# Six stretches of an attention and two-FFN kernel: instructions moved by a place or two

## Chip, core and metric

One core of a Trainium2 chip runs the whole program. The metric is the device time of one execution in microseconds (us), from the first to the last instruction with the launch's own share around it. The times of the kernel before are 1404.84, 1405.35 and 1405.74 us, median 1405.35.

## What is computed

The core of the reference, with B = 8 sequences of S = 512 tokens and 32 states, 8 heads of 64:

```python
scores = scale * x @ state.T;  a  = softmax(scores);  xread = a @ state
scores2 = scale * state @ x.T; a2 = softmax(scores2); sread = a2 @ x
x = concat([xread, sread]) as (4352 rows, 512)
h = silu(x @ w_gate) * (x @ w_val);  x = h @ w_out          # 1536 hidden columns
h = x @ w_in2;  g = max(h, 0) + alpha * min(h, 0)           # 2048 hidden columns
out = g @ w_out2
```

The weights come as float64 and are converted on the chip. Every product is made of three passes on a number's rounded high part and its remainder (`PASSES`: high times high, high times low, low times high), so each value that enters a product is first split: ScalarE copies it rounded (`acopy`, L78), then VectorE subtracts the copy from it (`sub_lo`, L84). A matmul here is 128x128 weights against 512 columns, or 256 for the states.

## The kernel before, in words

**Order of the work.** TensorE follows the order of the code everywhere. Up to the last token block the other engines and the DMA queue are ordered by the framework's planner, which goes by priority and its own costs, and by edges written by hand: `with tc.issue_after(ins)` puts what the block issues on the engine of `ins` behind `ins`. From the states' block on (L1265), VectorE, ScalarE, GpSimd and the SP queue follow the code too. Each engine works its queue in order.

**The attention and the first FFN.** The rows of one sequence are a block; the 256 state rows make a ninth, the states' block. Its inputs are read from attention by `second_read` (L217): 32 small matmuls into one of the two `aux` banks of PSUM. The product of state and weights (`state_times_w`, L508) also goes to the two `aux` banks and is split from there. `gate(f)` and `value(f)` are products for 128 hidden columns (12 of them, f = 0 to 11), in banks `g` and `v`; ScalarE reads `g` for the Silu (L547), VectorE multiplies by `v` (L551). `split(f)` (L554) makes the two parts, `project(f)` (L569) adds the result to the banks `acc0` to `acc3`.

For the first two blocks (XT = 2) all gates and values come first (the `order` loop, L769 to L792, with the list `extra` saying what is put after the gate or value of each number n), then a second loop (L809 to L821) splits and projects. Meanwhile `stream1` converts the weights in units. A unit has `act` (ScalarE, L268 and L269), `bits` (VectorE, L275 and L277, through a PSUM bank as scratch, then GpSimd L282 or L285) and, for w_out1, `uses` (the split into `wp`, L78 and L84). `banks` (L274) names the scratch bank: `acc0` and `acc1` for w_gate, w_val and the first three units of w_out1, `g` and `v` for the last three. Counting the steps, the fourth unit's `bits` are issued in the `order` loop, after the value products of the last number: half 0 after the first of its two values, half 1 after the second. The later units' are issued in the second loop.

**The states' block.** `ffn1` (L586) runs f = 0 to 11 with places (f, 0) after the gate, (f, 1) after the value and (f, 2) after the projection. For this block `split(f - 1)` stands at the head of f. `split_w(f + 2)` (L737), 1024 columns on ScalarE and VectorE, is at (f, 0). `x2_pair` (L907) prepares the inputs of the second FFN's first pair of blocks: four loads at (1, 2), four subtractions and seven 1024-column splits, two to a place, up to (6, 2).

**The second FFN.** It goes by pairs of blocks with seven products in place of eight (`FORMS`). A step t makes the seven products of one pair of hidden columns (`hidden_pair`, L974); after each comes a place (`fill`, L1217), which also takes one link of earlier steps: six matmuls of the output product (`project`, L1086, L1096). The first link into a sum is copied from its bank by ScalarE (L78, `sum<-acc`), the others are added by VectorE (L1107). A pair has ten such first links, in the steps t = 8p + 2 and 8p + 3 and the first place of 8p + 4. A link's bank is written again by the next link of its chain, two links later.

The first two steps are begun inside the states' block: two products for each f from `FROM` = 7 on, at (f, 0) and (f, 2), so ten of the fourteen; the other four follow the block's last projection. From f = `FROM` the block's own gate and value use `acc2` and `acc3`.

```python
copy = s == 0 and (pr, to, e) not in put_in
...
if copy:
    put_in.add((pr, to, e))
    acopy(r, o)
else:
    nc.vector.tensor_tensor(out=r, in0=o, in1=r, op=ALU.add)
```

Of the kernel before, what the change touches and what calls it, by code (L numbers as in the profile page):

```python
# [8 lines left out]
F32 = mybir.dt.float32  # L9
# [16 lines left out]
def attention_and_two_ffns(ctx: ExitStack, tc: tile.TileContext, x, state, w_gate, w_val,  # L26
# [220 lines left out]
    class Unit:  # L247
# [23 lines left out]
        def bits(self, i):  # L271
            m = self.m[i] = t2([P, HALF], I32, "m32")
            lo, hi = self.words(i)
            t = psum([P, HALF], self.banks[i]).bitcast(I32) if self.banks else m  # L274
            nc.vector.tensor_scalar(out=t, in0=hi, scalar1=0x0FFFFFFF, scalar2=3, op0=ALU.bitwise_and,  # L275
                                    op1=ALU.logical_shift_left)
            self.made = nc.vector.scalar_tensor_tensor(  # L277
                out=m, in0=hi, scalar=-0x80000000, in1=t, op0=ALU.bitwise_and, op1=ALU.bitwise_or)
            if self.place:
                o = self.place(i)  # L280
                n = o.shape[-1]
                nc.gpsimd.tensor_tensor(out=o.bitcast(I32), in0=m.rearrange("p (a n) -> p a n", n=n),  # L282
                                        in1=lo.rearrange("p (a n) -> p a n", n=n), op=ALU.add)
            else:
                nc.gpsimd.tensor_tensor(out=m, in0=m, in1=lo, op=ALU.add)  # L285
# [90 lines left out]
    def unit_w(j, c):  # L376

        def place(k):
            if j not in wraw:
                wraw[j] = t8([P, NPAIR, 2, 2 * P], F32, "wr")  # L380
            return wraw[j][:, c:c + 2, k, :]
        return Unit([words(w, c, c + 2, 2 * P * j, 2 * P * (j + 1)) for w in (w_gate, w_val)], place,
                    banks=("acc0", "acc1"))

    def unit_o(j):
        def take(i, m):
            if j not in wo1:
                wo1[j] = t8([P, 2, 2, DM], F32R, "wp")
            acopy(wo1[j][:, i, 0], m)
            sub_lo(wo1[j][:, i, 1], m, wo1[j][:, i, 0])  # L390
        return Unit([words(w_out1, 2 * j, 2 * j + 2, 0, DM)], take=take,
                    banks=("acc0", "acc1") if j < EARLY else ("g", "v"))
# [124 lines left out]
    class Block:  # L517
# [36 lines left out]
        def split(self, f):  # L554
            p = self.p.pop(f)
            t = self.hid[f] = t4([P, 2, S], F32R, "h")
            acopy(t[:, 0, :self.n], p)
# [28 lines left out]
    def ffn1(blk, slots, before):  # L586
# [5 lines left out]
        for f in range(NF1):  # L592
            if f and blk.n < S:
                blk.split(f - 1)
# [8 lines left out]
            elif before:  # L603
                before()
                if blk.n < S:
                    blk.start()
            fill(f, 2)
# [3 lines left out]
    with tc.manual_schedule(engines={mybir.EngineType.PE}):  # L611
# [67 lines left out]
        def ffn1_slots(b):  # L679
# [15 lines left out]
            if b == B - 1:  # L695
                put(0, 2, lambda: nc.sync.dma_start(alpha_sb, alpha.rearrange("(k p) -> p k", p=P)))
                gen = load_xs()
                for f in range(4, 8):
                    put(f, 0, lambda: next(gen))
                put(NF1 - 3, 1, lambda: split_w(0))  # L700
# [42 lines left out]

        blocks = [block(b) for b in range(B)]
# [10 lines left out]
        def columns(t):  # L755
            t.scores()
            with tc.issue_after(units1[3].made.ins):
# [5 lines left out]
                 2: [[att[0, g].second_scale for g in range(NG)], [att[0, 0].second_read],  # L763
                     [att[0, 1].second_read], []],
                 3: [[att[1, g].second_scale for g in range(NG)], [att[1, 0].second_read],
                     [att[1, 1].second_read], []]}
# [42 lines left out]
        for b in range(XT):  # L809
            for f in range(NF1):  # L810
# [3 lines left out]
                if b == 0:  # L814
                    with tc.issue_after(values[-1].ins):
# [90 lines left out]

        def x2_pair(pr):  # L907

            r, x = {}, x2.setdefault(pr, {})

            def load(c, d):
                r[d, c] = t4([P, 2, S], F32, "x2r")
                nc.sync.dma_start(r[d, c], x2d[2 * pr + c][:, 2 * d:2 * d + 2, :])

            def sub(o, x0, x1):
                nc.vector.tensor_tensor(out=o, in0=x0, in1=x1, op=ALU.subtract)

            def first():
                r["t1"] = t4([P, 2, S], F32, "x2t")
                sub(r["t1"], r[0, 1], r[0, 0])  # L920

            def put(k, src):
                x[k] = split8(r[src])

            return [lambda: [load(c, d) for d in range(2) for c in range(2)], first,
                    lambda: put("b00", (0, 0)),
                    lambda: sub(r[0, 0], r[1, 1], r["t1"]),
                    lambda: put("t2", (0, 0)), lambda: put("t1", "t1"),
                    lambda: sub(r[0, 1], r[1, 1], r[0, 1]),
                    lambda: put("t3", (0, 1)),  # L930
                    lambda: put("b10", (1, 0)),
                    lambda: sub(r[1, 0], r[1, 0], r[0, 0]),
                    lambda: put("t4", (1, 0)), lambda: put("b11", (1, 1))]
# [134 lines left out]
        acc, sums, put_in, giving, turning, sending, soon = {}, {}, set(), [], [], [], []  # L1068

# [16 lines left out]
        def project(gr, n, e):  # L1086
# [16 lines left out]
            if copy:  # L1103
                put_in.add((pr, to, e))
                acopy(r, o)
# [101 lines left out]
        def step(t, pr, s):  # L1207
# [7 lines left out]
            places = [0]  # L1215

            def fill():  # L1217
                places[0] += 1
                for e in list(sending):
# [42 lines left out]
        FROM = 7  # L1262
        forming, work = {}, [lambda: None for _ in range(2 * 7 + 1)]
        E = mybir.EngineType
        with tc.manual_schedule(engines={E.DVE, E.Activation, E.Pool, E.SP}):  # L1265


            slots = {}
            for f in range(2, NF1):
                slots.setdefault((f - 2, 0), []).append(lambda f=f: split_w(f))  # L1270
            for i, th in enumerate(x2_pair(0)):
                slots.setdefault((1 + i // 2, 2), []).append(th)
            slots.setdefault((4, 2), []).append(lambda: [ahead() for _ in range(3)])
# [10 lines left out]
            blk.split(NF1 - 1)  # L1284
# [42 lines left out]
```

## Time and profile before

| what | value |
|---|---|
| median of 3 runs | 1405.35 us (1404.84 to 1405.74) |
| profiled execution, its own time | 1406.81 us |
| span of its instructions | 1405.0 us |
| TensorE busy | 1361.7 us (97%) |
| VectorE busy | 1037.8 us (74%) |
| ScalarE busy | 827.5 us (59%) |
| GpSimd busy | 556.7 us (40%) |
| granted TensorE clock, mean | 0.993 |

The time of the profiled execution is 1.81 us more than its span, and 1.46 us more than the median. An engine that is busy for nearly the whole span sets the time; what can be won without changing its work is the time in which it waits, and the time in which it runs at the lower clock. In a timeline a row is a start, a duration, the engine, the line, the operation with the names of its output and inputs, how many such instructions in a row, and in brackets the engine's idle time before it with what ended that time. In a table of stretches the columns after the length are the busy us of TensorE, its weight loads, VectorE, ScalarE and GpSimd, each with its number of instructions, then the granted clock as a share of full speed.

### The profile page before, as it was taken

How to read it: one execution, taken by the hardware profiler on the slowest of the kernel's cores; microseconds unless marked ns; L12 is line 12 of the kernel's file. 1: busy time of each engine (PE TensorE's matmuls, PEld its weight loads, DVE VectorE, ACT ScalarE, POOL GpSimd, SP SyncE). 2: the span in 40 equal slices, each digit the busy share in tenths (PEclk: the TensorE clock that was granted, in tenths of full speed). 3: DMA queues.
4: the chain of work that ended last, by engine and by line, in shares of the span. 5: the costliest groups of instructions: out<-in, count | busy, mean ns of one | idle time of the engine just before them, and what ended most of it. 6: DMA issues, size and time to landing. Idle time of an engine off the chain costs nothing.

```text
span 1405.0 us, 20644 instructions
## 1 busy us (share of the span) xinstructions
PE 1361.7 (97%) x7238; PEld 1066.8 (76%) x7238; DVE 1037.8 (74%) x1593; ACT 827.5 (59%) x1440; POOL 556.7 (40%) x422
## 2 busy tenths in 40 slices
PE   6899999999999999999899999999999999999997
PEld 3566777777767677777897888878888888888886
DVE  6778535877777777765656789888897889888651
ACT  6756425555555555553456757776676667666642
POOL 3432111312222312320025666566566656656611
PEclk8999999999999999999999999999999999999999
DMA  9442333575757657533507688679868896886792
GB/s 299 158 138 49 85 78 91 160 183 160 208 135 222 173 138 210 153 113 105 190 21 254 181 303 273 199 205 327 291 201 226 299 314 224 218 263 219 266 316 94
DMA packets 274480, 271.92 MB, mean 194 GB/s; under 512 B 133960, under 2 KB 198472, under 8 KB 273352
## 3 DMA queue, kind: packets, MB, share of 16 engines
q1 hardware_dynamic: 272232, 270.21, 63.1%
q8 instruction: 57, 0.93, 0.3%
q10 hardware_dynamic: 2144, 0.39, 0.2%
q14 instruction: 47, 0.39, 0.1%
HBM read 206.05 MB, written 64.49 MB: 193 GB/s over the span
## 4 chain that ended last, share of the span: by engine, by line
PE 79%; DVE 7%; POOL 4%; issue 3%; ACT 3%; DMA 3%; SPq 0%; POOLq 0%; DVEq 0%; ACTq 0%
PE acc L1096 17%; PE acc L575 17%; PE g L534 9%; PE v L534 9%; PE v L984 7%; PE aux L984 5%; PE g L984 5%; PE aux L500 3%; POOL u L996 2%; PE acc L1166 2%; DVE h L84 1%; POOL u L953 1%; PE aux L163 1%; PE aux L223 1%; DMA wo<-ws2d 1%
## 5 line engine op out<-in xcount | busy, mean ns | idle before, releaser
L1096 PE MATMUL acc<-h,wo 128*128 128x512 f32 x1344 | 341.6, 390 | 2.6 <-ACT sum L78 1.5
L575 PE MATMUL acc<-h,wp 128*128 128x512 f32 (+1 forms) x1296 | 298.1, 380 | 7.3 <-DVE h L84 5.3
L1096 PEld LDWEIGHTS acc<-h,wo 128*128 128x128 f32 x1344 | 251.2, 188 | 56.8 <-ACT sum L78 2.7
L575 PEld LDWEIGHTS acc<-h,wp 128*128 128x128 f32 x1296 | 235.0, 189 | 57.5 <-DVE h L84 7.3
L953 POOL TENSOR_TENSOR u<-u,m 128x512 f32<-128x512 f32 x96 | 128.7, 1341 | 300.1 <-ACT m L952 267.8
L84 DVE TENSOR_TENSOR h<-u,h 128x512 fp32r<-128x512 f32 x160 | 151.6, 964 | 24.1 <-ACT h L78 23.8
L534 PE MATMUL g<-a,sw 128*128 128x512 f32 x576 | 153.7, 401 | 3.6 <-ACT h L78 1.7
L78 ACT ACTIVATE h<-u 128x512 fp32r<-128x512 f32 x160 | 100.2, 630 | 89.3 <-POOL u L996 88.0
L534 PE MATMUL v<-a,sw 128*128 128x512 f32 x576 | 151.5, 398 | 0.7 <-DVE p L551 0.5
L534 PEld LDWEIGHTS g<-a,sw 128*128 128x128 f32 x576 | 103.9, 188 | 62.2 <-issue 33.5
L984 PE MATMUL v<-x,w 128*128 128x512 f32 x576 | 146.5, 390 | 0.1
L1107 DVE TENSOR_TENSOR sum<-acc,sum 128x512 f32<-128x512 f32 x184 | 125.4, 682 | 22.7 <-PE acc L1096 21.9
L534 PEld LDWEIGHTS v<-a,sw 128*128 128x128 f32 x576 | 105.2, 188 | 32.9 <-issue 8.9
L984 PEld LDWEIGHTS v<-x,w 128*128 128x128 f32 x576 | 107.8, 188 | 22.7 <-DVE u L992 0.5
L84 DVE TENSOR_TENSOR h<-h,h 128x512 fp32r<-128x512 f32 (+1 forms) x80 | 79.2, 991 | 42.4 <-ACT h L78 40.0
L317 POOL TENSOR_TENSOR m<-m,raw 128x512 int32<-128x512 int32 x32 | 46.3, 1447 | 156.4 <-DVE m L315 115.7
L996 POOL TENSOR_TENSOR u<-u,u 128x512 f32<-128x512 f32 x64 | 105.5, 1648 | 5.0
L84 DVE TENSOR_TENSOR sw<-aux,sw 128x512 fp32r<-128x512 f32 x96 | 62.7, 684 | 57.6 <-ACT sw L78 57.4
L78 ACT ACTIVATE sw<-aux 128x512 fp32r<-128x512 f32 x96 | 52.6, 595 | 86.6 <-PE aux L500 79.3
L952 ACT ACTIVATE m<-m,alpha_sb 128x512 f32<-128x512 f32 (+1 forms) x144 | 99.2, 689 | 0.0
L984 PE MATMUL g<-x,w 128*128 128x512 f32 x384 | 97.7, 390 | 0.7 <-ACT h L951 0.7
L984 PE MATMUL aux<-x,w 128*128 128x512 f32 x384 | 97.6, 390 | 0.0
(158 smaller groups left out, 2098.8 us busy)
## 6 DMA issues: line engine op xcount, KB each, us to landing
wo<-ws2d SPq DMA_DIRECT2D x224, 256.0 KB, 5.1
w<-w2d SPq DMA_DIRECT2D x104, 512.0 KB, 5.4
w2d<-sp SPq DMA_DIRECT2D x32, 512.0 KB, 4.0
x2r<-x2d SPq DMA_DIRECT2D x25, 512.0 KB, 5.8
w<-w2d SPq DMA_DIRECT2D x48, 256.0 KB, 5.5
x2d<-xo SPq DMA_DIRECT2D x32, 256.0 KB, 2.6
raw<-in_moe_w_in_dram SPq DMA_DIRECT2D x16, 512.0 KB, 4.0
raw<-in_moe_w_out_dram SPq DMA_DIRECT2D x16, 512.0 KB, 4.7
```

Source lines behind the costliest of these rows:

```text
L78: return nc.scalar.activation(o, i, AF.Copy)
L84: (eng or nc.vector).tensor_tensor(out=o, in0=src, in1=hi.bitcast(F32), op=ALU.subtract)
L317: nc.gpsimd.tensor_tensor(out=m, in0=m, in1=lo, op=ALU.add)
L500: nc.tensor.matmul(self.o[Ns * c:Ns * (c + 1), :], stt[b][q, 2 * c + g, :], wraw[j][q, c].rearrange("p k f -> p (k f)"), start=True, stop= ...
L534: nc.tensor.matmul(o[:, :self.n], self.lhs(f, k, a, which), self.rhs(k, c), start=(i == 0), stop=(i == last))
L575: nc.tensor.matmul(self.acc[e][:, :self.n], wo1[f // 2][:, f % 2, a, e * P:(e + 1) * P], t[:, c, :self.n], start=(self.n == S and f == 0 a ...
L952: nc.scalar.activation(n, n, AF.Copy, scale=alpha_sb[:, f:f + 1])
L953: nc.gpsimd.tensor_tensor(out=out, in0=out, in1=n, op=ALU.add)
L984: nc.tensor.matmul(o, w[:, a, q], x[k][:, q, e], start=start and n == 0, stop=stop and n == 5, skip_group_check=True)
L996: nc.gpsimd.tensor_tensor(out=o, in0=x0, in1=x1, op=ALU.subtract)
L1096: nc.tensor.matmul(o, w[:, f, a, e], h[:, q], start=first and i == 0, stop=i == 5, skip_group_check=True)
L1107: nc.vector.tensor_tensor(out=r, in0=o, in1=r, op=ALU.add)
```

## The change

Six stretches are touched, named here by the order of the run.

1. Second reads: for n = 2 and 3 of the first loop, the two `second_read` stand one entry later in `extra`.
2. Conversion banks: `banks` becomes a function of the half, asked when `bits` is issued. For w_out1 it gives `acc0` and `acc1` as long as the first block has no accumulators, else `g` and `v`.
3. Conversion order: in the second loop, what a conversion step issues on ScalarE goes behind the rounded copy of that turn's `split(f)`.
4. States' block: the four loads go to place (5, 0) of the last token block and the four subtractions to (7, 2) to (10, 2) there, with three tiles more; the seven splits stand one to a place, (0, 2) to (6, 2); `split_w(f + 2)` goes from (f, 0) to (f, 1); `split(f)` goes from the head of f + 1 to before (f, 2); the first loads of w2 go from (4, 2) to (3, 2).
5. First products: `FROM` is 6, so twelve of the fourteen products of the first two steps are inside the states' block.
6. First sums' copies: those in places 4 to 7 of a step go to VectorE (five of a pair's ten, twenty in all).

```diff
-            t = psum([P, HALF], self.banks[i]).bitcast(I32) if self.banks else m
+            t = psum([P, HALF], self.banks(i)).bitcast(I32)
...
-                    banks=("acc0", "acc1"))
+                    banks=lambda i: f"acc{i}")
...
-                    banks=("acc0", "acc1") if j < EARLY else ("g", "v"))
+                    banks=lambda i: f"acc{i}" if blocks[0].acc is None else ("g", "v")[i])
...
-            acopy(t[:, 0, :self.n], p)
+            self.rounded = acopy(t[:, 0, :self.n], p)
...
         for f in range(NF1):
-            if f and blk.n < S:
-                blk.split(f - 1)
             blk.gate(f)
...
+            if blk.n < S:
+                blk.split(f)
             fill(f, 2)
...
+                put(5, 0, first_load)
+                for i in range(4):
+                    put(7 + i, 2, lambda i=i: first_sub(i))
...
+        def first_load():
+            for d in range(2):
+                for c in range(2):
+                    raw0[f"b{d}{c}"] = t4([P, 2, S], F32, "x2r")
+                    nc.sync.dma_start(raw0[f"b{d}{c}"], x2d[c][:, 2 * d:2 * d + 2, :])
+
+        def first_sub(i):
+            x0, x1, to = (("b01", "b00", "t1"), ("b11", "t1", "t2"), ("b11", "b01", "b01"), ("b10", "t2", "t4"))[i]
+            o = raw0[to] if to in raw0 else t4([P, 2, S], F32, "x2t")
+            nc.vector.tensor_tensor(out=o, in0=raw0[x0], in1=raw0[x1], op=ALU.subtract)
+            raw0["t3" if to == "b01" else to] = o
...
-                 2: [[att[0, g].second_scale for g in range(NG)], [att[0, 0].second_read],
-                     [att[0, 1].second_read], []],
+                 2: [[att[0, g].second_scale for g in range(NG)], [], [att[0, 0].second_read],
+                     [att[0, 1].second_read]],
...
                 if b == 0:
-                    with tc.issue_after(values[-1].ins):
+                    with tc.issue_after(values[-1].ins), tc.issue_after(blocks[b].rounded.ins):
                         stream1.until(2 * NJ1 + f // 2, 2)
...
-                acopy(r, o)
+                (vcopy if where[0] > 3 else acopy)(r, o)
...
-        FROM = 7
+        FROM = 6
...
             for f in range(2, NF1):
-                slots.setdefault((f - 2, 0), []).append(lambda f=f: split_w(f))
-            for i, th in enumerate(x2_pair(0)):
-                slots.setdefault((1 + i // 2, 2), []).append(th)
-            slots.setdefault((4, 2), []).append(lambda: [ahead() for _ in range(3)])
+                slots.setdefault((f - 2, 1), []).append(lambda f=f: split_w(f))
+            for i, k in enumerate(FORMS):
+                slots.setdefault((i, 2), []).append(lambda k=k: x2[0].update({k: split8(raw0.pop(k))}))
+            slots.setdefault((3, 2), []).append(lambda: [ahead() for _ in range(3)])
```

(The entry of n = 3 is changed like that of n = 2; `where[0]` is the place of the step, set in `fill`; `x2_pair` is taken out.)

## Rows read from the trace of the kernel before

**Rows 1.** The page, part 1: busy time of the engines, whole run.

```profile
PE 1361.7 (97%) x7238; PEld 1066.8 (76%) x7238; DVE 1037.8 (74%) x1593; ACT 827.5 (59%) x1440; POOL 556.7 (40%) x422
```

**Rows 2.** TensorE's waits: waiting line, releaser, total us, times, longest us.

```profile
PE aux L155 <- DMA xn<-in_x_dram: 7.9, 4, 5.4
PE acc L575 <- DVE h L84: 5.3, 5, 3.2
PE aux L223 <- DVE sw L84: 3.0, 2, 1.5
```

**Rows 3.** Timeline round the first second read, VectorE and TensorE.

```profile
59.83 1.29 DVE L84 TENSOR_TENSOR sw<-aux,sw 128x512 fp32r<-128x512 f32 x2 [0.95 <-ACT sw L78]
60.58 0.66 PE L223 MATMUL aux<-xn,e2t 128*32 128x64 f32 x32 [1.48 <-DVE sw L84]
```

**Rows 4.** Timeline, VectorE and TensorE round conversion of w_out1's fourth unit.

```profile
126.98 0.68 DVE L277 SCALAR_TENSOR_TENSOR m<-raw,g 128x512 int32<-128x512 int32 x1
...
127.80 1.62 PE L534 MATMUL g<-a,sw 128*128 128x512 f32 x6 [1.67 <-ACT h L78]
...
130.64 16.48 PE L575 MATMUL acc<-h,wp 128*128 128x512 f32 x72
...
134.58 0.68 DVE L277 SCALAR_TENSOR_TENSOR m<-raw,v 128x512 int32<-128x512 int32 x1
```

**Rows 5.** Timeline, ScalarE and TensorE in the first block's projections.

```profile
147.69 0.63 ACT L78 ACTIVATE wp<-m 128x512 fp32r<-128x512 f32 x1 [2.26 <-POOL m L285]
148.22 3.89 ACT L78 ACTIVATE h<-p 128x512 fp32r<-128x512 f32 x7
...
148.89 0.50 PE L575 MATMUL acc<-h,wp 128*128 128x512 f32 x1 [1.76 <-ACT h L78]
149.70 20.72 PE L575 MATMUL acc<-h,wp 128*128 128x512 f32 x83 [0.30 <-DVE h L84]
```

**Rows 6.** Stretches of 25 us: busy us (instructions), clock, DMA share, GB/s.

```profile
150.00:175.00 25.00, 25.00 (x103) 19.61 (x102) 14.14 (x24) 10.61 (x18) 1.42 (x1) 0.93 0.19 64
...
675.00:700.00 25.00, 20.80 (x169) 20.20 (x168) 17.26 (x22) 12.96 (x20) 0.00 (x0) 1.00 0.70 236
...
1025.00:1050.00 25.00, 25.00 (x112) 20.72 (x111) 24.21 (x31) 15.72 (x26) 19.34 (x13) 1.00 0.73 218
```

**Rows 7.** Timeline, states' block: VectorE, then TensorE.

```profile
683.09 1.23 DVE L916 TENSOR_TENSOR x2t<-x2r,x2r 128x1024 f32<-128x1024 f32 x1 [4.40 <-DMA x2r<-x2d]
684.23 0.42 DVE L84 TENSOR_TENSOR h<-s,h 128x256 fp32r<-128x256 f32 x1
684.56 1.22 DVE L84 TENSOR_TENSOR ws<-wr,ws 128x1024 fp32r<-128x1024 f32 x1
...
684.70 1.58 PE L575 MATMUL acc<-h,wp 128*128 128x256 f32 x11 [3.16 <-DVE h L84]
...
699.22 1.58 PE L575 MATMUL acc<-h,wp 128*128 128x256 f32 x11 [0.91 <-DVE h L84]
```

**Rows 8.** Timeline, TensorE from the first products to the first sums.

```profile
724.38 1.58 PE L575 MATMUL acc<-h,wp 128*128 128x256 f32 x11 [0.73 <-DVE h L84]
...
750.33 1.67 PE L984 MATMUL g<-x,w 128*128 128x512 f32 x6 [0.74 <-ACT h L951]
...
755.18 0.73 PE L1096 MATMUL acc<-h,wo 128*128 128x512 f32 x2 [0.88 <-DVE h L84]
```

**Rows 9.** Timeline, first sums of the first two pairs, TensorE and VectorE.

```profile
771.25 1.65 PE L1096 MATMUL acc<-h,wo 128*128 128x512 f32 x6 [0.35 <-ACT sum L78]
...
923.11 0.89 DVE L84 TENSOR_TENSOR h<-u,h 128x512 fp32r<-128x512 f32 x1 [1.69 <-ACT h L78]
...
925.41 1.66 PE L1096 MATMUL acc<-h,wo 128*128 128x512 f32 x6 [1.14 <-ACT sum L78]
```

**Rows 10.** The page, part 5: VectorE groups, count, busy us, mean ns, idle.

```profile
L84 DVE TENSOR_TENSOR h<-u,h 128x512 fp32r<-128x512 f32 x160 | 151.6, 964 | 24.1 <-ACT h L78 23.8
...
L1107 DVE TENSOR_TENSOR sum<-acc,sum 128x512 f32<-128x512 f32 x184 | 125.4, 682 | 22.7 <-PE acc L1096 21.9
```

More of the change, by code (lines that the diff above doesn't have):

```diff
@@ L742, in split_w @@
             ws[f] = t
+        raw0 = {}
+        def first_load():
[8 more added lines that the diff above has]
+            raw0["t3" if to == "b01" else to] = o
         blocks = [block(b) for b in range(B)]
@@ L762, in attention_and_two_ffns @@
                  1: [[v.first_scale], [u.first_parts], [v.first_parts], []],
-                 2: [[att[0, g].second_scale for g in range(NG)], [att[0, 0].second_read],
-                     [att[0, 1].second_read], []],
-                 3: [[att[1, g].second_scale for g in range(NG)], [att[1, 0].second_read],
-                     [att[1, 1].second_read], []]}
+                 2: [[att[0, g].second_scale for g in range(NG)], [], [att[0, 0].second_read],
+                     [att[0, 1].second_read]],
+                 3: [[att[1, g].second_scale for g in range(NG)], [], [att[1, 0].second_read],
+                     [att[1, 1].second_read]]}
         order = [(0, 0), (0, 1), (1, 0), (1, 1)] + [(b, j) for j in range(2, NJ1) for b in range(XT)]
@@ L905, in x2_forms @@
             return places
[L907 to L933, printed above, removed]
         def x2_last():
@@ L1068, in attention_and_two_ffns @@
         acc, sums, put_in, giving, turning, sending, soon = {}, {}, set(), [], [], [], []
+        where = [0]
         def store(u, o):
@@ L1215, in step @@
             places = [0]
+            where[0] = 0
             def fill():
                 places[0] += 1
+                where[0] = places[0]
                 for e in list(sending):
@@ L1268, in attention_and_two_ffns @@
             slots = {}
+            x2[0] = {}
             for f in range(2, NF1):
-                slots.setdefault((f - 2, 0), []).append(lambda f=f: split_w(f))
-            for i, th in enumerate(x2_pair(0)):
-                slots.setdefault((1 + i // 2, 2), []).append(th)
-            slots.setdefault((4, 2), []).append(lambda: [ahead() for _ in range(3)])
+                slots.setdefault((f - 2, 1), []).append(lambda f=f: split_w(f))
+            for i, k in enumerate(FORMS):
+                slots.setdefault((i, 2), []).append(lambda k=k: x2[0].update({k: split8(raw0.pop(k))}))
+            slots.setdefault((3, 2), []).append(lambda: [ahead() for _ in range(3)])
             first = (_ for t in range(2) for _ in step(t, *STEPS[t]))
@@ L1283, in attention_and_two_ffns @@
             ffn1(blk, slots, lambda: blocks[B - 1].finish(B - 1))
-            blk.split(NF1 - 1)
             blk.finish(B)
```

## The prediction

> **What bounds it now.** I read the page first: TensorE is busy for 1361.7 of 1405.0 us [rows 1]. The change neither adds nor takes away a matmul, so it can win only from TensorE's 43 idle us and from time at the lower clock. The second view is therefore TensorE's list of waits. Its largest entry, 7.9 us for the first loads of x, lies at the start, which the change leaves alone; the projections' wait for VectorE (5.3 us in five) and the second reads' (3.0 us in two) lie where it moves things [rows 2]. Third, the timeline at each such wait, to see which instruction the late one stood behind in its queue. VectorE and ScalarE are seldom full, so these are questions of order: a short instruction that TensorE needs stands behind a long one that could wait.
>
> **Part 1, second reads.** The read writes an `aux` bank. Both banks hold the states' products until VectorE has split them, 1.29 us for two from 59.83; TensorE stands 1.48 us before the read at 60.58 [rows 3], and as long again for the second sequence (3.0 us in two [rows 2]). With the reads one place later, a gate product of 1.6 us (its like in [rows 4]) runs in that gap: the products before end some 59.1 (60.58 less 1.48), the gate then ends at 60.6, and the first bank is free about 60.5, half-way through the two splits. The read becomes as late as the bank, so I keep 0.03 us of each wait: 2.9 us won, between 0 and 2.96. The value products after it need nothing that comes later than before.
>
> **Part 2, conversion banks.** Only the fourth unit of w_out1 gets other banks, since `bits` of the later ones come when the accumulators exist. Its first half has its scratch in `g`, between two gates: VectorE reads `g` until 127.66 (126.98 and 0.68) and the gate starts at 127.80 after 1.67 us [rows 4]. The profile names ScalarE's copies as the releaser; by the end times it is VectorE. In `acc0` that half no longer stands in the gate's way: 1.67 us won. The bound on the other side is the second half: today it ends at 135.26 (134.58 and 0.68) after the last value. In `acc1` it has to end before the first projection writes that bank, three matmuls of 0.23 us (16.48 by 72) after a start that moves to 128.97, so at 129.66. If the planner leaves it where it is, TensorE waits 5.6 us. I take 1.67, because the unit's data are ready long before and its bank is then free; 5.6 is the first rival.
>
> **Part 3, conversion order.** At 146 to 150 TensorE waits 1.76 and 0.30 us for the seventh turn's split. ScalarE makes that copy only at 148.22, in a run of seven, directly after a conversion copy at 147.69 that itself waited 2.26 us for GpSimd [rows 5]. Seven copies in a row mean that their buffers had long been free. The edge puts each turn's copy ahead of that turn's conversion instructions: 2.06 us won, between 0 and 2.06. What the edge makes later is the last unit's `act` and the `uses` of three units. They have room: the last of these copies was made at 147.69, and the first projection that needs its unit is the eleventh, four turns of 2.75 us (12 by 0.229) after the seventh, which stood at 148.89 [rows 5].
>
> Behind this wait the granted clock falls: 0.93 over 150 to 175 and 103 matmuls, where a full-speed stretch of the same length shows 112 of the like size [rows 6]. That is 7% of 25 us, 1.75 us at 1.2 in place of 2.4 GHz, and I take 1.7 as won with the wait, between 0 and 1.75. Against it: after the wait of 3.16 us at 681 the stretch shows a clock of 1.00 [rows 6, 7], so not every pause of this length costs clock. The Trainium skill (TensorE: Matmul & The Clock Gate, Part 1) says the gate looks at activity in a window that runs on its own, whatever the kernel does. By that, a pause may or may not cost the clock as it happens to lie; the rows agree, and the sum would be 1.7 us less well off if one of the pauses that stay met it.
>
> **Part 4, states' block.** TensorE waits 3.16 us at 684.70 for a split that VectorE does at 684.23, behind a subtraction that had waited 4.40 us for the four loads; at 699.22 it waits 0.91 us for the same chain of subtraction and splits [rows 7]. With loads and subtractions in the last token block, nothing here waits for a transfer. What VectorE has to do between two projections is then a multiplication and a split (0.42 each), one `ws` split and one pair split (1.22 each) [rows 7]: 3.3 us, against three products of about 1.45 us, 4.3 us. The needed split stands ahead of the pair's. 4.07 us won, between 0 and 4.07. The four subtractions, 1.23 us each, and four loads move into the last token block, where TensorE has no wait; I cost them at nothing. Their cover is that block's slack, and they hold seven of sixteen tiles to the end of it. On the SP queue they now stand before stores of converted weights; the wait of the w2 loads stays the same, since both they and their first product move up by one turn.
>
> **Part 5, first products.** Three waits follow the start of the second FFN: 0.73 us at 724.38 (a split queued behind ScalarE's work on a new product), then 0.74 at 750.33 and 0.88 at 755.18, where the last four of the fourteen products run without anything between them and ScalarE falls behind [rows 8]. Split before place (f, 2) removes the first kind there; with two products in place of four at the end the other two go. But a split still stands behind the products at (f, 0), and in the last turn that is again a product with ScalarE's three activations. I keep one wait of 0.73 for it: 1.62 us won of 2.35.
>
> **Part 6, first sums' copies.** TensorE waits 0.35 us at 771.25 and 1.14 at 925.41 for copies in ScalarE's queue [rows 9]. On VectorE the copy stands behind the split that ends at 924.00 (923.11 and 0.89); with 0.68 for the copy, as a sum from PSUM takes [rows 10], it ends at 924.68 at the latest, 0.7 us ahead of today. ScalarE, free of two copies, lets that split be earlier too. I take 0.9 of 1.14 and the whole 0.35: 1.25 us. Eighteen of the twenty moved copies meet no wait and are worth nothing; they add 0.68 us each to VectorE. Their cover is VectorE's slack: in the stretch from 1025 on, where it takes every sum, TensorE is busy throughout [rows 6].
>
> **Sum.** 2.9 + 1.67 + 2.06 + 1.7 + 4.07 + 1.62 + 1.25 = 15.3 us. The span goes from 1405.0 to 1389.7 and the profiled execution's time from 1406.81 to 1391.5. The median of the runs lies 1.46 below that execution: 1390.0.
>
> **The rivals.**
> - *The second half of the fourth unit comes late* (part 2): 5.6 us of wait in the first projection, 1395.6. For it: the planner orders VectorE by its own costs. Against it: nothing holds that half back but its bank. 0.07.
> - *The order in the second loop stays bad* (part 3), because conversions that now start later are awaited later: the wait and its clock stay, 3.8 us, 1393.8. 0.10.
> - *The gate's wait is ScalarE's*, as the profile says, and the bank edit does nothing: 1391.7. 0.05.
> - *A pause that remains costs the clock*: 1391.7. The windowed rule is that of the page named above. 0.06.
> - *The last token block pays*: with seven tiles held, its own splits wait for a buffer and what part 4 wins comes back there, 1394.1. For it: sixteen tiles serve weights, splits and loads alike. Against it: a split needs its buffer for two turns only. 0.06.
> - *Slower: VectorE becomes the bound in the first sums* (part 6). All other parts win 14.05 us; with twenty copies moved, the kernel is slower from 0.70 us per copy that reaches TensorE. A VectorE instruction that meets GpSimd takes 0.96 on the mean [rows 10]; at that, twenty cost 19.3 us and the time is 1410.6. Against it: between 1025 and 1050 VectorE is busy for 24.21 of 25 us and TensorE for all 25.00 [rows 6]. 0.03. The Trainium skill (SBUF — State Buffer, "SBUF: two separate sides") lets VectorE and GpSimd block each other only where VectorE has two SBUF inputs or a two-port mode; a copy from PSUM has neither. By that rule the copy costs its 0.68 and this rival falls; [rows 10] agree, 682 ns for the sums with one input in PSUM against 964 for the splits with both in SBUF.
>
> **How the numbers follow.** The forecast has 0.63. With all the waits of these stretches and their clock gone, the sum is 16.4 us, and some pauses nearby of a few tenths may go too: low end 1387. The high end, 1396.5, takes in the first five rivals and two of the smaller ones together. A measurement of this kernel tells about 0.2% from no change, 2.8 us: faster means under 1402.5. The forecast and the first five rivals are all on that side (0.97); I leave 0.04 of it for several of them together, and for waits that the planner's new order might make in the blocks between 185 and 650 us, which no row here prices: 0.93 faster, 0.04 the same, 0.03 slower.
>
> **What would show it.** TensorE's wait before the second reads below 0.2 us; no VectorE conversion in `g` between the last gates; the rounded copies spread out, not seven in a run; clock 1.00 from 150 on; no subtraction left in the states' block and no wait of TensorE over 1 us there; no wait of the links for a copy. It would be wrong if a wait of over 2 us stood in the last token block or at the first projection, or if VectorE's copies held up a link.

## The result, and the profile after

The changed kernel takes 1392.53 us (median of 4 runs, 1392.1 to 1393.28), the kernel before 1405.37 beside it: a ratio of 0.9906, interval 0.9892 to 0.992. The prediction was 1390.0 with a range of 1387.0 to 1396.5, so the direction and the range held. The profiled execution takes 1392.94 us, with a span of 1391.2, against 1406.81 and 1405.0: 13.8 us of span won where the sum said 15.3 (13.87 by the traces, before rounding).

The page of the changed kernel, part 1, answers to [rows 1]:

```profile
PE 1357.8 (98%) x7238; PEld 1065.4 (77%) x7238; DVE 1048.1 (75%) x1613; ACT 818.8 (59%) x1420; POOL 557.3 (40%) x422
```

TensorE has 33 us idle in place of 43, and 4 us less of busy time for the same matmuls. The twenty copies have gone from ScalarE to VectorE. TensorE's waits (waiting line, releaser, total us, times, longest us), beside [rows 2]:

```profile
PE acc L575 <- DVE h L84: 2.0, 2, 1.1
...
PE acc L1086 <- DMA wo<-ws2d: 1.3, 1, 1.3
...
PE acc L1086 <- DVE sum L1097: 1.2, 1, 1.2
```

The row of the second reads is gone, the projections' waits are 2.0 us in two in place of 5.3 in five, and the links now wait for a DMA, which they did not before. The timeline of TensorE in the changed kernel shows where these lie (the last number before the bracket is how many instructions; line 1086 was 1096 before):

```profile
60.12 0.65 PE L223 MATMUL aux<-xn,e2t 128*32 128x64 f32 x32
...
121.47 1.65 PE L534 MATMUL v<-a,sw 128*128 128x512 f32 x6 [0.59 <-DVE p L551]
...
125.71 35.52 PE L575 MATMUL acc<-h,wp 128*128 128x512 f32 x156
...
628.09 2.79 PE L575 MATMUL acc<-h,wp 128*128 128x512 f32 x11 [1.10 <-DVE h L84]
...
731.78 1.58 PE L575 MATMUL acc<-h,wp 128*128 128x256 f32 x11 [0.86 <-DVE h L84]
...
740.11 1.62 PE L1086 MATMUL acc<-h,wo 128*128 128x512 f32 x6 [1.28 <-DMA wo<-ws2d]
...
909.94 1.65 PE L1086 MATMUL acc<-h,wo 128*128 128x512 f32 x6 [0.54 <-DVE sum L81]
...
927.74 1.65 PE L1086 MATMUL acc<-h,wo 128*128 128x512 f32 x6 [1.17 <-DVE sum L1097]
```

The read at 60.12 has no wait [rows 3], the 156 matmuls at 125.71 run in one piece where there were two breaks [rows 5], and between 661 and 731 nothing is left of the waits of 3.16 and 0.91 us [rows 7]. New are 0.59 us among the last gates, 1.10 in the last token block and 1.28 at the first link. At the second pair's first links 0.54 and 1.17 stand where the kernel before has 1.14 [rows 9] and a small one. That one, and a small wait in the last turn of the states' block that is gone, stand so in the trace of before:

```profile
742.14 1.58 PE L575 MATMUL acc<-h,wp 128*128 128x256 f32 x11 [0.25 <-DVE h L84]
...
942.34 1.66 PE L1096 MATMUL acc<-h,wo 128*128 128x512 f32 x6 [0.21 <-DVE sum L1107]
```

The table of stretches shows the clock behind the seventh turn at full speed, against 0.93 in [rows 6]:

```profile
150.00:175.00 25.00, 25.00 (x142) 19.28 (x140) 13.71 (x26) 8.91 (x15) 2.72 (x3) 1.00 0.19 64
```

**Six stretches.** To see what each part is worth I cut the run at starts of TensorE's instructions, which no wait inside a stretch can blur: the fourth and sixth products of states and weights (L500; 57.52 and 75.08 in the changed kernel), the first projection (125.71), the first transform of the third sequence (L163, 161.16), the first gate of the states' block (660.94), its seventh link (756.54; the row at 771.25 in [rows 9]) and the transposes of the last sums (1322.02). What lies ahead of the first cut takes 56.6 to 59.5 us in all runs, as the first loads of x come, and is left out.

| run, us | second reads | last gates | projections | token blocks | to the 7th link | to the last sums |
|---|---|---|---|---|---|---|
| before | 20.18 | 52.44 | 39.71 | 498.10 | 102.80 | 564.82 |
| changed | 17.56 | 50.63 | 35.45 | 499.78 | 95.60 | 565.48 |
| changed, again | 17.55 | 50.62 | 35.45 | 499.78 | 95.98 | 565.06 |
| reads back | 20.15 | 50.60 | 35.45 | 499.90 | 95.72 | 565.00 |
| banks back | 17.56 | 52.10 | 35.46 | 499.84 | 95.81 | 565.23 |
| order back | 17.56 | 50.87 | 35.48 | 499.76 | 96.24 | 565.31 |
| banks and order back | 17.56 | 52.43 | 38.09 | 499.66 | 95.53 | 565.84 |
| split back | 17.57 | 50.60 | 35.45 | 499.79 | 100.53 | 565.07 |
| loads back | 17.56 | 50.61 | 35.45 | 498.22 | 95.90 | 564.87 |
| first products back | 17.56 | 50.62 | 35.46 | 499.66 | 95.46 | 564.09 |
| copies back | 17.56 | 50.61 | 35.46 | 499.72 | 96.11 | 564.84 |
| three back (mixed) | 17.56 | 50.64 | 35.45 | 498.42 | 96.47 | 564.71 |
| output weights early | 17.55 | 50.62 | 35.45 | 499.94 | 94.04 | 565.04 |
| gate behind copy | 17.55 | 50.64 | 35.45 | 499.22 | 96.05 | 564.92 |

Six of these runs have the same code from the states' block on (changed, again, reads, banks, order, both back). They spread over 95.53 to 96.24 and 565.00 to 565.84, so in the last two columns less than 0.8 us tells nothing; in the others the like runs agree within 0.3. Each run has two to four executions, and apart from both back and split back the intervals of their ratios overlap that of the changed kernel. What is concluded below therefore rests on these columns and on the rows, which are of one execution each.

From before to after, by columns: 2.62, 1.81 and 4.26 won, 1.68 lost, 7.20 won, 0.66 lost; with 0.50 ahead of the first cut and 0.19 lost behind the last that is the span won, 13.87 but for rounding.

### The profile page after: what moved, and what is told of

The parts are those of the page before. It is cut to its first block, busy times and chain, and to the rows that moved or that the text cites. A ratio compares the mean times of both kernels' runs of the same rounds, so it can differ in the third digit from the quotient of the medians.

```text
span 1391.2 us, 20653 instructions
## 1 busy us (share of the span) xinstructions
PE 1357.8 (98%) x7238; PEld 1065.4 (77%) x7238; DVE 1048.1 (75%) x1613; ACT 818.8 (59%) x1420; POOL 557.3 (40%) x422
## 4 chain that ended last, share of the span: by engine, by line
PE 84%; DVE 5%; DMA 3%; POOL 2%; issue 2%; ACT 2%; SPq 1%; DVEq 0%; POOLq 0%; ACTq 0%
PE acc L575 19%; PE acc L1086 18%; PE v L534 10%; PE g L534 9%; PE v L973 8%; PE aux L973 5%; PE g L973 5%; PE aux L500 3%; PE acc L1156 2%; PE acc L534 1%; DVE h L84 1%; DMA wo<-ws2d 1%; POOL u L985 1%; PE aux L163 1%; POOL u L942 1%
```

## The experiments

Each undoes one move in the changed kernel, unless it says otherwise.

**Second reads back.**

```diff
-                 2: [..., [], [att[0, 0].second_read],
-                     [att[0, 1].second_read]],
+                 2: [..., [att[0, 0].second_read],
+                     [att[0, 1].second_read], []],
```

(and the same for n = 3)

> The changed kernel with part 1 alone undone: the second reads stand where they stood. Theory (aux banks): both waits of 1.48 us before the reads return, and each delays TensorE by a little more than the idle shown, so the time rises by 2.8 to 3.3 us, to about 1395.5. Rival (the planner): the other engines' order is laid anew, and the time moves by under 1 us or by an amount that no wait before the reads explains.

Measured: 1394.89 us, ratio 0.992 (0.9905 to 0.9935); the first column is 2.59 longer, a little under the 2.8 to 3.3 expected, and no other moves. The row of the wait stands as in [rows 3]:

```profile
59.68 0.65 PE L223 MATMUL aux<-xn,e2t 128*32 128x64 f32 x32 [1.48 <-DVE sw L84]
```

Part 1 stands by itself and is worth 2.6 us.

**Conversion banks back.**

```diff
-  banks=lambda i: f"acc{i}" if blocks[0].acc is None else ("g", "v")[i]
+  banks=lambda i: f"acc{i}" if j < EARLY else ("g", "v")[i]
```

> The changed kernel with part 2 alone undone: the fourth unit of w_out1 has its scratch in g and v again. Theory (VectorE's scratch blocks the bank): the gate's wait of 1.67 us returns and the time rises by 1.5 to 2.0 us, to about 1394.3. Rival (the gate waited for ScalarE's copies, as the profile's row named them): no change within 0.5 us.

Measured: 1394.98 us, ratio 0.992 (0.9905 to 0.9935); the second column is 1.47 longer, just under the 1.5 to 2.0 expected, and the third stays. TensorE, then VectorE, in the timeline of this run:

```profile
124.24 1.61 PE L534 MATMUL g<-a,sw 128*128 128x512 f32 x6 [1.57 <-ACT h L78]
...
123.41 0.68 DVE L277 SCALAR_TENSOR_TENSOR m<-raw,g 128x512 int32<-128x512 int32 x1
```

The profile again names ScalarE, but only a bank was changed, and the gate starts 0.15 us after VectorE's read of `g` ends (124.09). The rival that the wait is ScalarE's falls.

**Conversion order back.**

```diff
-  with tc.issue_after(values[-1].ins), tc.issue_after(blocks[b].rounded.ins):
+  with tc.issue_after(values[-1].ins):
```

> The changed kernel with part 3 alone undone: conversions no longer stand behind the rounded copy. Theory: the wait before the seventh projection returns (1.8 to 2.5 us) and the granted clock falls behind it (1.7 us more), so the time rises by 3.5 to 4.3 us, to about 1396.5, with a clock of 0.92 to 0.94 in one stretch of 25 us. Rival 1: the wait returns without the clock, 2 to 2.5 us. Rival 2: with the fourth unit's banks changed, the order takes care of itself: no change within 0.5 us.

Measured: 1393.3 us, ratio 0.9913 (0.9895 to 0.9932); the third column stays at 35.48 and no wait stands in it, as the second rival had it. The second column is 0.24 longer, where the runs with nothing changed there agree within 0.04. By this run alone part 3 is worth next to nothing, though its wait was in the trace of before and is gone. So it had to be asked together with its neighbour:

**Banks and order back**, both edits above at once.

> The changed kernel with parts 2 and 3 both undone, since neither alone brought the wait in the projections back. Theory (either edit frees the seventh turn's copy: with the fourth unit converted early nothing awaits it, and with the edge nothing can stand ahead of it): the stretch from the first projection to the next block's first product grows from 35.5 us back to about 39.7, with the waits of 1.76 and 0.30 us and a clock of 0.93 in one stretch of 25 us; the stretch before it grows by 1.5 us. Rival (the copy comes in time because everything before it runs 2.6 us earlier, by part 1): the stretch stays at 35.5.

Measured: 1399.4 us, ratio 0.9949 (0.9926 to 0.9971). The third column is 2.64 longer. TensorE, ScalarE, and the table of stretches of this run, beside [rows 5] and [rows 6]:

```profile
145.45 0.50 PE L575 MATMUL acc<-h,wp 128*128 128x512 f32 x1 [1.79 <-ACT h L78]
146.26 19.08 PE L575 MATMUL acc<-h,wp 128*128 128x512 f32 x83 [0.30 <-DVE h L84]
...
144.78 3.89 ACT L78 ACTIVATE h<-p 128x512 fp32r<-128x512 f32 x7
...
150.00:175.00 25.00, 25.00 (x113) 19.87 (x111) 12.05 (x23) 9.03 (x15) 2.48 (x2) 1.00 0.19 64
```

The run of seven copies and both waits are back. Either edit alone frees the seventh copy. With the order and the old banks the third column is 35.46, and the copies stand between the conversions. With the banks and the old order it is 35.48: the last conversion copy starts at 142.24 there, where it starts at 144.25 with both back, and the planner puts copies between the conversions by itself. Undoing one of two sufficient cures shows neither. And the clock stays at 1.00 here: the 83 matmuls take 19.08 us where in [rows 5] they take 20.72. The same wait costs 2.64 us in one execution and 4.26 in the other. The other two executions of this run took 1.7 and 1.8 us longer than the profiled one; what their clock did behind the wait is not known.

**Split of the states' block back to the head of the next turn.**

```diff
+            if f and blk.n < S:
+                blk.split(f - 1)
             blk.gate(f)
...
-            if blk.n < S:
-                blk.split(f)
             fill(f, 2)
...
             ffn1(blk, slots, lambda: blocks[B - 1].finish(B - 1))
+            blk.split(NF1 - 1)
```

> The changed kernel with one piece of part 4 undone: the states' block's split stands at the head of the next turn again, the rest of part 4 stays. Theory (the split needs to stand ahead of the work at the third place): waits of 0.5 to 1 us return in the turns in which a product's three ScalarE instructions stand at that place, 1 to 2.5 us in all between the states' block's first gate and the first link. Rival (only the loads and subtractions mattered): under 0.3 us.

Measured: 1398.75 us, ratio 0.9944 (0.9921 to 0.9966); 4.93 us longer to the seventh link, where 1 to 2.5 were expected. TensorE, ScalarE and the table of stretches round the block's last turn:

```profile
736.58 0.38 PE L575 MATMUL acc<-h,wp 128*128 128x256 f32 x1 [2.09 <-ACT h L78]
737.90 2.64 PE L575 MATMUL acc<-h,wp 128*128 128x256 f32 x11 [0.94 <-DVE h L84]
740.34 2.06 PE L973 MATMUL v<-x,w 128*128 128x512 f32 x6
...
735.50 0.72 ACT L941 ACTIVATE m<-m,alpha_sb 128x512 f32<-128x512 f32 x1
736.12 0.41 ACT L78 ACTIVATE h<-s 128x256 fp32r<-128x256 f32 x1
...
725.00:750.00 25.00, 21.46 (x112) 18.22 (x111) 13.58 (x18) 13.37 (x26) 10.32 (x8) 0.93 0.34 114
```

The copy stands behind the three activations of a first product. Not all of the 4.93 us are waits: the clock falls to 0.93 behind them, where the changed kernel shows 1.00. The eleven matmuls after the wait take 2.64 us for 1.58 at full speed and the six behind them 2.06 for 1.55, so some 1.6 us are the clock's, in this one execution, and 3.3 the waits'. The 3.16 us at 684 do not come back, though the split is late again: the loads are still out of the way.

**Loads and subtractions back in the states' block.**

```diff
-                put(5, 0, first_load)
-                for i in range(4):
-                    put(7 + i, 2, lambda i=i: first_sub(i))
...
-            for i, k in enumerate(FORMS):
-                slots.setdefault((i, 2), []).append(lambda k=k: x2[0].update({k: split8(raw0.pop(k))}))
+            for i, th in enumerate(x2_pair(0)):
+                slots.setdefault((1 + i // 2, 2), []).append(th)
```

(the seven splits go back with them, two to a place)

> The changed kernel with the other piece of part 4 undone: the four loads and four subtractions are in the states' block again, the early split stays. Theory: the projection's wait for the subtraction behind the loads returns, 3.0 to 4.5 us between the states' block's first gate and the first link; and the wait of 1.10 us in the last token block goes, 1.3 us less between the third block and the states' block. In sum 1.7 to 3.2 us slower. Rival (the early split lies ahead of the subtraction, so the transfer is covered): under 1 us in the states' block, and the kernel is no slower.

Measured: 1391.4 us, ratio 0.989 (0.9862 to 0.9919), so not slower, as the rival had it. The token blocks take 1.56 less and the way to the seventh link is as long as in the changed kernel (95.90). VectorE waits for the load as it did in [rows 7]:

```profile
673.34 1.23 DVE L930 TENSOR_TENSOR x2t<-x2r,x2r 128x1024 f32<-128x1024 f32 x1 [3.56 <-DMA x2r<-x2d]
```

TensorE has no wait behind it. So the 3.16 us also had two sufficient cures, the early split and the early loads, and the loads are the one that costs something. (The two were not undone together; that the wait then stands is read from the kernel before.) Where it is paid shows on ScalarE round 624 us, first in the changed kernel:

```profile
623.94 1.06 ACT L78 ACTIVATE ws<-wr 128x1024 fp32r<-128x1024 f32 x1 [1.93 <-POOL m L317]
625.32 0.60 ACT L547 ACTIVATE s<-g 128x512 f32<-128x512 f32 x1 [0.32 <-PE g L534]
625.81 0.62 ACT L78 ACTIVATE h<-s 128x512 fp32r<-128x512 f32 x1
```

and with the loads back:

```profile
623.67 1.07 ACT L78 ACTIVATE ws<-wr 128x1024 fp32r<-128x1024 f32 x1 [1.94 <-POOL m L317]
624.64 0.61 ACT L78 ACTIVATE h<-s 128x512 fp32r<-128x512 f32 x1
625.16 0.62 ACT L78 ACTIVATE sp<-m 128x512 fp32r<-128x512 f32 x1
625.68 0.58 ACT L547 ACTIVATE s<-g 128x512 f32<-128x512 f32 x1
```

With the loads in this block the planner puts the next turn's Silu (L547) ahead of the copy `h` that TensorE needs, and ScalarE even waits 0.32 us for that gate first. One more run asks whether this exchange is the cause:

**Gate behind the copy**: the changed kernel, with that one order put back.

```diff
-            blk.gate(f)
+            if f and blk.n == S:
+                with tc.issue_after(blk.rounded.ins):
+                    blk.gate(f)
+            else:
+                blk.gate(f)
```

> The changed kernel with one order put back in the token blocks: the gate's Silu of a turn is issued behind the rounded copy of the turn before, which in the last token block is the one place where the two stand the other way round. Theory (the 1.10 us wait of the last token block is that exchange on ScalarE): no wait stands there, and the stretch from the first token block's second projection to the states' first gate takes 498.2 to 498.5 where it takes 499.78. Rival (the exchange is only the sign of a late product by GpSimd, which would be late as before): the stretch keeps 499.5 or more.

Measured: 1391.78 us, ratio 0.9889 (0.9869 to 0.9908); the token blocks take 499.22. The theory missed, and so did the rival: 0.56 of the 1.56 us is won. TensorE in this run:

```profile
625.70 3.22 PE L575 MATMUL acc<-h,wp 128*128 128x512 f32 x12
...
631.84 0.63 PE L739 MATMUL aux<-ident,xsn 128*128 128x128 f32 x4 [0.31 <-DMA xsn<-srd]
```

The wait of 1.10 is gone, but twelve matmuls still take 3.22 us where they take 2.88 with the loads back: VectorE makes two 1024-column weight splits in a row (2.64 us) ahead of the needed one here, and one with the loads back. And a wait for a transfer comes out, 0.48 us from start to start. SP shows its queue:

```profile
621.35 2.45 SPq L757 DMA_DIRECT2D x2r<-x2d  x3
623.85 0.48 SPq L735 DMA_DIRECT2D xsn<-srd  x1
```

That read of 256 KB is issued behind three of the moved loads, of 512 KB each. With the loads back it is issued later, at 627.52, and nothing waits for it. So the loads cost by three orders at once (ScalarE, VectorE, SP); the first one is shown, the other two are read from the trace.

**First products back.**

```diff
-        FROM = 6
+        FROM = 7
```

> The changed kernel with part 5 alone undone: FROM is 7 again, so four of the fourteen products follow the block. The prediction's term: the waits at the first steps return, 1.2 to 2 us more between the states' block's first gate and the second link. Theory formed since (the change has put other waits there, 0.86 for a split and 1.28 for the output weights' transfer): under 0.7 us.

Measured: 1393.09 us, ratio 0.9902 (0.9874 to 0.9931). To the seventh link nothing changes beyond the spread; TensorE, then VectorE and GpSimd:

```profile
736.20 1.65 PE L973 MATMUL g<-x,w 128*128 128x512 f32 x6 [0.68 <-ACT h L940]
...
741.04 0.73 PE L1086 MATMUL acc<-h,wo 128*128 128x512 f32 x2 [0.89 <-DVE h L84]
...
923.06 1.83 POOL L942 TENSOR_TENSOR u<-u,m 128x512 f32<-128x512 f32 x1 [2.54 <-ACT m L941]
...
923.08 2.35 DVE L84 TENSOR_TENSOR h<-u,h 128x512 fp32r<-128x512 f32 x2
```

The waits of 0.74 and 0.88 us [rows 8] come back as 0.68 and 0.89, and those of 0.86 and 1.28 at 731.78 and 740.11 go. One pair was exchanged for another. The last column is 0.9 us below the lowest of the six like runs. Where this run has the two rows of GpSimd and VectorE, the changed kernel shows:

```profile
923.53 1.30 POOL L942 TENSOR_TENSOR u<-u,m 128x512 f32<-128x512 f32 x1 [2.54 <-ACT m L941]
...
923.68 3.41 DVE L84 TENSOR_TENSOR h<-u,h 128x512 fp32r<-128x512 f32 x2
```

The two splits take 2.35 us on VectorE when they start with GpSimd's instruction, which is then the long one (1.83), and 3.41 when they start 0.15 us behind it; the second wait of the pair (1.17 at 927.74) stands behind that. The Trainium skill (SBUF — State Buffer, "SBUF: two separate sides") has a VectorE instruction with two SBUF inputs and a GpSimd instruction take one pair of ports in turn, the first to start for its whole length. The changed kernel's rows agree; in the other two GpSimd's row starts 0.02 us ahead and is yet the one held up, an offset too small to say by these rows which came first. Over all 160 such splits of the changed kernel the rule is borne out: 58 meet no GpSimd instruction and take 0.68 us on the mean, 88 start more than 0.03 us behind one and take 1.16, and nine start more than 0.03 us ahead of one and take 0.68.

At this place GpSimd starts 0.07 to 0.17 us first in all thirteen other runs. One of them is the mixed run below, which has `FROM = 7` too and whose last column is 564.71. So the 0.9 us cannot be put down to the move; an offset of a tenth seems to decide, which no count of instructions gives. The offset was not tried by itself.

**First sums' copies back on ScalarE.**

```diff
-                (vcopy if where[0] > 3 else acopy)(r, o)
+                acopy(r, o)
```

> The changed kernel with part 6 alone undone: all first sums are copied by ScalarE. The prediction's term: waits of 0.35 and 1.14 us return, the time rises by 1.2 to 1.8 us, to about 1394. Theory formed since (VectorE is what is short in the second pair's first steps, so the copies there only move the wait): no change within 0.5 us; the waits at the second pair are 1.1 to 1.4 us in all, against 1.93 in the changed kernel, and the first pair's wait of 0.35 is back.

Measured: 1391.87 us, ratio 0.9899 (0.9884 to 0.9913), not slower than the changed kernel. TensorE at the seventh link, which waited 0.35 us before [rows 9], and at the second pair's first links:

```profile
756.13 1.52 PE L1086 MATMUL acc<-h,wo 128*128 128x512 f32 x6
...
910.07 1.66 PE L1086 MATMUL acc<-h,wo 128*128 128x512 f32 x6 [1.13 <-ACT sum L78]
...
927.28 1.63 PE L1086 MATMUL acc<-h,wo 128*128 128x512 f32 x6 [0.50 <-DVE sum L1097]
```

The 0.35 us are gone without the copies, though the theory had them back. In the second pair 1.13 and 0.50 stand where the changed kernel has 0.54 and 1.17, more than the 1.1 to 1.4 expected in all: the wait moves from one link to the next.

**Output weights early**: the changed kernel, with the first three loads of output weights issued before the last turn of the states' block.

```diff
-                for n in range(3):
-                    load_wo(t // 2, n)
+                if t > 1:
+                    for n in range(3):
+                        load_wo(t // 2, n)
...
+            slots.setdefault((NF1 - 1, 0), []).append(lambda: [load_wo(0, n) for n in range(3)])
```

> The changed kernel with the first three loads of output weights issued before the last turn of the states' block instead of at its end, ahead of the queue's stores and other weights. Theory (the 1.28 us wait at the first link is the transfer of these weights and nothing is close behind it): that wait is gone, and the states' first gate to link 2 is 1.3 to 1.5 shorter than the changed kernel's 84.72. Rival (VectorE's second sums or splits come as late): a wait of DVE stands at the link in its place, and under 0.4 us is won.

Measured: 1390.96 us, ratio 0.9883 (0.9863 to 0.9903). No wait is left at the first link, and to the third link it takes 83.16 us in place of 84.72, 1.56 less, a little over the 1.3 to 1.5 expected:

```profile
737.93 1.52 PE L1086 MATMUL acc<-h,wo 128*128 128x512 f32 x6
```

The wait was the transfer's, with nothing close behind it.

**Three moves taken back** (loads, first products, and the copies of all pairs but the first), the diffs above together, with

```diff
-                (vcopy if where[0] > 3 else acopy)(r, o)
+                (vcopy if where[0] > 3 and pr == 0 else acopy)(r, o)
```

> The changed kernel with three of its moves taken back: the second reads' loads and subtractions stand in the states' block again, the first products follow the eighth turn's end again (FROM = 7), and the first sums' copies go to VectorE for the first pair of tokens only. The early splits, the places of the second reads, the conversion banks and the orders stay. Theory (each of the three costs time where the single runs showed it): the last token block 498.2 us as with the loads back, from the states' first gate to link 112 about 385.0 to 385.8, where the changed kernel takes 387.35; 1.6 from the token block and 1.5 to 2.3 from the states' block, so 3.1 to 3.9 us under the changed kernel, near 1388.9. Rival (the moves lean on each other: without the late sums' place the copies of the second pair wait elsewhere): under 2.0 us below the changed kernel.

and **the changed kernel again** beside it:

> The changed kernel itself, beside the mixed version on one chip, so that the two are measured against the same runs of the kernel before. Its stretches should come out as in its first profile within 0.3 us each (17.6, 50.6, 35.4, 499.8, 79.2), and its time within 1.5 us of 1392.5.

Measured: mixed 1392.13 us, ratio 0.9891 (0.9876 to 0.9905); changed again 1393.56, ratio 0.9905 (0.9888 to 0.9921). The changed kernel's stretches return within 0.42 us (0.3 was expected), the wait for the output weights being 1.66 us this time. The mixed version is 1.4 us faster by the medians, with overlapping intervals, not 3.1 to 3.9: the rival held. The token blocks give their 1.36, but in the states' block and the second pair TensorE shows:

```profile
687.60 1.69 PE L534 MATMUL g<-xs,ws 128*128 128x256 f32 x12 [0.64 <-ACT s L547]
...
909.91 1.66 PE L1111 MATMUL acc<-h,wo 128*128 128x512 f32 x6 [1.16 <-ACT sum L78]
```

The gains of single runs did not add.

The lowest time measured is that of the version with the output weights early, 2.6 us under the changed kernel by the medians on the same chip (the intervals overlap; the removed wait accounts for 1.6 to 2). Together with the loads back it was not run.

## Why the prediction was right, and where it was off

- **Part 1** was right: 2.62 us for 2.9. A wait's idle time in the profile is not exactly what its removal gives: 2.96 of idle gave 2.62 here, and 2.09 gave 2.64 in part 3.
- **Part 2** was right in cause and size, 1.81 us for 1.67 (1.47 when undone), and the reading of the end times against the profile's label was tested. The first rival (5.6 us at the first projection) did not come: 156 matmuls run without a break.
- **Part 3** was right in the sum, 4.26 us for the two waits and the clock where 3.76 were forecast, and its step holds: with the banks back, the edge alone keeps the wait away. But part 2's banks alone do so too, so the edge is not needed beside them. The prediction priced the parts one by one as if each wait had one cure.
- **The clock** was won as said (1.62 us, 39.71 less 38.09, for 1.7), but it is no fixed price of the wait: the same wait, three microseconds earlier in another run, left the clock at 1.00. Whether that is its position or changes from one execution to the next is not shown. The prediction had the doubt in its text and took the full value; for the profile of before that was right.
- **Part 4** failed in the step "I cost them at nothing" and in "the needed split stands ahead of the pair's" as the gain of both moves together. Beside the early split (4.93 us to the seventh link when undone, some 1.6 of it clock), the moved loads and subtractions bring nothing there, and they cost 1.56 in the last token block. The rival that this block pays was right in place and in that TensorE waits; its reason (splits waiting for a buffer) was not what stands in the trace, which shows a planner that orders three engines differently.
- **Part 5** was mis-sized: nothing to the seventh link for 1.62. The kept wait came (0.86 for the 0.73 forecast), and what the prediction did not look for is the next thing in line behind the two waits that go: the transfer of the output weights, 1.28 us, issued when the states' block ends. It looked at what would hold the products, not at what the link itself needs.
- **Parts 4, 5 and the first pair's copy together** were forecast at 6.04 us (4.07, 1.62, 0.35) and gave 7.20, with a new wait of 1.28 in it. The sum went by the waits of [rows 7] and [rows 8]. The kernel before has also a wait of 0.25 us at 742.14 and three pauses of 0.2 to 0.3 us (ahead of 697.92 and 746.57, and in the row at 731.44); these four, 1.4 us from start to start, are gone too. What the rest of part 4 (the places of `split_w` and of the weights' loads) gives was not tried alone.
- **Part 6** failed: of 0.90 us forecast in the second pair nothing shows, neither between the two profiles (0.66 longer, within the spread) nor when it is undone. The step that failed looks at one link alone, with the copy's end on VectorE 0.7 us earlier "at the latest": that wait does fall, from 1.14 to 0.54, and the next link then waits 1.17 for VectorE where it waited 0.21. So one of the prediction's signs of being wrong came, a link held up by VectorE's copy (0.54 at 909.94; L81 is that copy). The slower rival, VectorE as the bound, did not come. Its 0.96 us was misread: that is the mean of all 160 splits of [rows 10], of which 61 meet no GpSimd instruction and take 0.68, and the other 99 take 1.14. The moved copies take 0.67 to 0.69 each.
- **The total.** Of the 2.5 us between 1390.0 and 1392.5, 1.4 are the sum (1391.5 forecast for the profiled execution, 1392.94 measured). The rest is the offset: that execution lay 1.46 us above the median before and 0.41 after. That the sum came so near is in part luck: 0.5 too little for part 3 and 1.16 for the states' block stand against 1.68 in the token blocks, taken as nothing, and 0.9 that the second pair did not give.

## What to carry to other kernels

When two moves each stand ahead of the same late instruction, undo them singly and together: a move that shows nothing alone can be the spare of another, and then only the cheaper one is worth keeping. A transfer or a subtraction that is moved into an idle-looking block still changes the order that a planner gives every engine there, so price it by that block's own critical copies. Before counting a wait as won, look up all that the waiting instruction needs (the weights' transfer too) and how late the next one is.

## What was not expected of the chip

The granted clock after a wait of the same kind (1.76 and 0.30 us in one run, 1.79 and 0.30 in the other) was 0.93 in one stretch and 1.00 in the other, with 20.72 and 19.08 us for the same 83 matmuls. Behind 3.16 us it was 1.00 [rows 6, 7], behind 2.09 and 0.94 it was 0.93. A wait's length does not tell whether it costs clock. And two splits took 3.41 us where they start 0.15 us behind a GpSimd instruction and 2.35 where they start within 0.02 us of it.
